# Attention and gated dense block on one core: the exponential table, the last dense bank, two score blocks and the output stores change their places

## The chip, the cores and the metric

The kernel runs on one core of a Trainium2 chip. The metric is the time of one execution in device microseconds, as the median of several runs. The profile comes from one further execution of the same program. The engines are called TensorE (PE; PEld is its weight load), VectorE (DVE), ScalarE (ACT), GpSimd (POOL) and SyncE (SP, which here only issues transfers).

## What is computed

S = 2048 tokens, D = 512 channels, 32 heads of 16 channels, a hidden width F = 1376, all in 32-bit floats:

```python
xn = layernorm(x)
q, k, v = split_heads(xn @ wqkv)             # 32 heads of 16
p = softmax(q @ k.T / 4)                      # 2048 x 2048 a head
s = merge_heads(p @ v) @ wo
g = silu(gelu(xn @ w1 + b1, approximate) @ w2 + b2)
return x + s * g
```

Products with the weights are made from operands split into a high part (rounded to the format of TensorE's fast 32-bit mode) and a low part, in three matmuls each; q and k are stored in both parts too.

## The kernel before

**Units, blocks and steps.** Heads are handled in 8 groups of four (`NG`, `GH`), queries in 4 chunks of 512 (`NCH`); a *unit* `u` is one group with one chunk, 32 in all. The softmax needs each query's maximum before its exponentials. So every unit is passed twice: a max pass, in which TensorE makes 64 *score blocks* of 128 queries x 512 keys (L193) and VectorE reduces each (L199), and an attention pass of 16 *steps*, one for each 128 keys. A step makes four tiles of transposed scores (L714, letters T), turns them into exponentials on ScalarE (one tile each by L717, two together by L719), and adds the value products of the step before (L785, letter V). Of the 2048 score blocks, `SOON` are made in the dense stage and the rest in the attention steps, three in most of them. `due(n)` (L939) says how many are to be done after step `n`; its term `min(FEW, n // 16)` drops one block in the first step of each of the first `FEW` units.

**The dense stage** comes ahead of the attention steps. An order written out by a small planner (`plan`) goes through value tiles (`first`), halves of pairs of units (`half`: two blocks of the first dense layer or of q and k, L583), and parts of the second dense layer (`down`, whose four banks `PA` add up over a chunk of 512 tokens). A half ends with `evac`: ScalarE takes the banks (L368 with the activation function, L370 without, for q and k), rounds them to the high part (L374), and GpSimd subtracts for the low part. The pairs end with a q-k pair, behind which three `down` parts remain. `fill` (L559) puts the score blocks between the matmuls (*rows*): a block may come when `row >= 2 * FILL0 + APART * made`, up to `SOON`.

**The hand-over.** Before the last but one `down` part ScalarE loads the table with the exponential (L731); before the last part TensorE makes the four score tiles of step 0 early (L735). After the last part VectorE adds b2 to the four banks of the last chunk in the order 0, 2, 1, 3 (L643), and GpSimd stores them to `g_d`. Banks 0 and 2 then serve the double tile `two`, bank 1 the value products `pv`, bank 3 the tile `pst` of the later steps. The orders of the first two steps stand in L999; step 1 is `TSTTSVT`.

**The attention steps** take their operation letters from `ORDER`, `FIRST` and `TWO` (S, X and Y are score blocks, H and W parts of the output projection). Work of other engines hangs on step numbers by `at(n, function, ...)`: the key loads by GpSimd (`load_k`, L121), the maxima (L246 to L276), and behind each unit `o_move` (copies the unnormalised output and denominators by SyncE), `o_den` (reciprocal, store of the denominators to `den_d`, and their load back, spread over rows, to `dn`, L813 to L817) and `o_div` (GpSimd multiplies, L823). Each queue goes in program order: an instruction of SyncE or GpSimd that waits holds up all behind it. Key buffers go round three groups (`KB`): group 3 gets the buffer of group 0 and is loaded in halves at steps 56 to 61 and 64 to 69. In group 3's first unit the max pass goes through the keys chunk by chunk.

**The output projection** begins at step `DONE` = 493, beside the last attention steps. Tokens are taken in tiles of 128; tiles 0 to 9 (`NW`; called *tokens* 0 to 9 in the code) go in pairs of two, every four steps: `w_two` splits two channel blocks into `oh` and `ol` (L890 or L892, L893), `w_halves` multiplies with Wo (L912), `load_gx` fetches g and x of a tile (L841, L842), `gate` makes the sigmoid by tanh (L846, L847), `w_gate` and `w_add` (L918, L923) finish, and SyncE stores to `out` (L924). The first ten tiles share four buffers `gx`; a load waits until the tile that had the buffer before is stored. Tiles 10 to 15 have places of their own and come after the last step.

## Time and profile before

| what | us |
|---|---|
| median of 3 runs | 1549.02 (1548.08 to 1549.08) |
| the profiled execution | 1548.39 |
| its span, first to last instruction | 1546.6 |
| VectorE's maxima (L199), 2048 of 687 ns | 1318.0 busy |
| value products (L785), 4096 matmuls | 543.4 busy |
| wide exponentials (L719), 511 of 1018 ns | 520.1 busy |
| first attention steps | from about 469 |
| output projection | from about 1467 |

A row of a timeline has the start, the duration (both us), the engine, the line, the operation, what is written and read, how many instructions are merged in the row, and in brackets the idle time of the engine before it with what ended it. A row of the chain that ended last has start, duration and what the time was spent in. Durations of neighbours overlap, since the engines pipeline; the spacing of starts is what a row costs. A row of a table by stretches has the busy us (and count) of PE, PEld, DVE, ACT and POOL, then the granted TensorE clock as a share of full speed, the DMA share and GB/s.

### The profile page before, as it was taken

How to read it: one execution, taken by the hardware profiler on the slowest of the kernel's cores; microseconds unless marked ns; L12 is line 12 of the kernel's file. 1: busy time of each engine (PE TensorE's matmuls, PEld its weight loads, DVE VectorE, ACT ScalarE, POOL GpSimd, SP SyncE). 2: the span in 40 equal slices, each digit the busy share in tenths (PEclk: the TensorE clock that was granted, in tenths of full speed). 3: DMA queues.
4: the chain of work that ended last, by engine and by line, in shares of the span. 5: the costliest groups of instructions: out<-in, count | busy, mean ns of one | idle time of the engine just before them, and what ended most of it. 6: DMA issues, size and time to landing. Idle time of an engine off the chain costs nothing.

```text
span 1546.6 us, 31293 instructions
## 1 busy us (share of the span) xinstructions
PE 1540.3 (100%) x12232; PEld 923.3 (60%) x12232; DVE 1417.6 (92%) x2295; ACT 1211.8 (78%) x1881; POOL 366.2 (24%) x370
## 2 busy tenths in 40 slices
PE   9999999999999999999999999999999999999999
PEld 8889999999995444444444444444444444444456
DVE  7699999999998999999999999999999999999945
ACT  4333433333329999999999999999999999999984
POOL 4235575756741002001000100100010000000143
PEclk9999999999999999999999999999999999999999
DMA  6525443454432113113311411411041111110153
GB/s 211 154 59 149 124 144 102 128 161 132 137 90 66 41 33 71 33 37 54 67 33 33 71 35 39 63 40 30 22 82 29 33 30 30 43 30 21 48 189 127
DMA packets 78643, 116.83 MB, mean 76 GB/s; under 512 B 28036, under 2 KB 28292, under 8 KB 77320
## 3 DMA queue, kind: packets, MB, share of 16 engines
q1 hardware_dynamic: 74748, 101.89, 23.3%
q0 software_dynamic: 3264, 12.35, 4.7%
q8 instruction: 96, 1.57, 0.4%
q10 hardware_dynamic: 484, 0.60, 0.1%
q14 instruction: 51, 0.42, 0.1%
HBM read 84.35 MB, written 25.97 MB: 71 GB/s over the span
## 4 chain that ended last, share of the span: by engine, by line
PE 97%; DVE 1%; DMA 1%; ACT 0%; SPq 0%; POOL 0%; issue 0%; POOLq 0%; DVEq 0%
PE pv L785 32%; PE ps L193 22%; PE ps L583 13%; PE two L714 8%; PE sp L583 5%; PE pst L714 4%; PE ps L714 4%; PE pst L583 3%; PE pv L583 2%; PE ps L912 1%; PE ps L92 1%; PE ps L455 1%; PE pv L487 1%; PE pst L92 0%; DMA den_d<-dr 0%; PE two L92 0%
## 5 line engine op out<-in xcount | busy, mean ns | idle before, releaser
L199 DVE TENSOR_REDUCE mx<-ps 128x2 f32<-128x512 f32 x2048 | 1318.0, 687 | 69.8 <-PE ps L193 20.5
L785 PE MATMUL pv<-slot,vsb 128*32 128x512 f32 x4096 | 543.4, 604 | 0.0
L719 ACT ACTIVATE slot<-two 128x1024 f32<-128x1024 f32 x511 | 520.1, 1018 | 0.0
L193 PEld LDWEIGHTS ps<-kt,slot 48*128 48x128 f32 x1358 | 212.8, 184 | 291.8 <-DVE mx L199 280.1
L193 PE MATMUL ps<-kt,slot 48*128 48x256 f32 (+1 forms) x1358 | 377.3, 365 | 0.0
L717 ACT ACTIVATE slot<-ps 128x512 f32<-128x512 f32 x515 | 307.6, 598 | 15.7 <-PE ps L714 6.2
L717 ACT ACTIVATE slot<-pst 128x512 f32<-128x512 f32 x511 | 309.0, 605 | 0.6 <-PE ps L714 0.6
L583 PE MATMUL ps<-slot,w1h 64*128 64x512 f32 x1088 | 224.4, 392 | 0.0
L193 PE MATMUL ps<-kt,qz 48*128 48x512 f32 x512 | 202.0, 395 | 0.0
L714 PE MATMUL two<-qt,kt 50*128 50x512 f32 x766 | 197.8, 395 | 0.5 <-DVE gt L643 0.3
L714 PE MATMUL ps<-qt,kt 50*128 50x512 f32 x387 | 189.8, 492 | 0.0
L193 PEld LDWEIGHTS ps<-slot,slot 48*128 48x128 f32 x590 | 92.8, 184 | 123.2 <-DVE mx L199 118.2
L193 PE MATMUL ps<-slot,slot 48*128 48x256 f32 (+1 forms) x590 | 165.4, 366 | 0.0
L785 PEld LDWEIGHTS pv<-slot,vsb 128*32 128x32 f32 x4096 | 81.6, 108 | 132.1 <-issue 124.3
L583 PEld LDWEIGHTS ps<-slot,w1h 64*128 64x128 f32 x1088 | 153.5, 185 | 9.7
L714 PE MATMUL pst<-qt,kt 50*128 50x512 f32 x383 | 156.0, 407 | 0.0
L583 PE MATMUL ps<-slot,w1l 64*128 64x512 f32 x544 | 155.8, 392 | 0.0
L375 POOL TENSOR_TENSOR hl<-hg,hh 128x512 fp32r<-128x512 f32 x76 | 96.7, 1295 | 158.5 <-ACT hh L374 117.1
L368 ACT ACTIVATE hg<-ps,b_sb 128x512 f32<-128x512 f32 x44 | 27.9, 685 | 132.8 <-PE ps L583 121.5
L714 PEld LDWEIGHTS two<-qt,kt 50*128 50x128 f32 x766 | 114.7, 186 | 1.7 <-DVE gt L643 0.7
L193 PEld LDWEIGHTS ps<-kt,qz 48*128 48x128 f32 x512 | 93.7, 183 | 0.9 <-DVE mx L199 0.5
L246 POOL CAST mh<-nt 128x32 fp32r<-128x32 f32 x19 | 4.0, 211 | 361.5 <-DVE nt L244 334.9
(194 smaller groups left out, 1962.5 us busy)
## 6 DMA issues: line engine op xcount, KB each, us to landing
raw<-in_w SPq DMA_DIRECT2D x88, 256.0 KB
qk_h<-hh SPq DMA_DIRECT2D x32, 256.0 KB
qk_l<-hl SPq DMA_DIRECT2D x32, 256.0 KB
qt<-qk_h SPq DMA_DIRECT2D x128, 64.0 KB
slot<-qk_h SPq DMA_DIRECT2D x92, 64.0 KB
g_d<-gt POOLq DMA_DIRECT2D x16, 256.0 KB, 3.3
qt<-qk_l SPq DMA_DIRECT2D x64, 64.0 KB
dn<-den_d SPq DMA_DIRECT2D x32, 128.0 KB
```

The lines of the kernel that those rows point to most:

```text
L92: nc.tensor.matmul(ps, lhs[a], rhs[b], start=first and n == 0, stop=last and n == 2)
L193: return nc.tensor.matmul(ps[:, c0:c0 + w], QS[u][r, p, qi * P:(qi + 1) * P], kts[u // NCH % KB][p][r, k0:k0 + w], start=True, stop=True).ins
L199: nc.vector.tensor_reduce(MX[u][:, 2 * p:2 * p + 2, qi, ki][:, heads, parts], ps.rearrange("p (n c) -> p n c", c=HC), axis=AX.X, op=OP.max)
L368: nc.scalar.activation(raw, ph.pop(u), AF.Gelu_apprx_tanh, bias=b1_sb[:, u[2]:u[2] + 1])
L375: nc.gpsimd.tensor_sub(hl, raw, hh.bitcast(F32))
L455: nc.tensor.matmul(pq["q", g, c], W1[g][i][:, k * P:(k + 1) * P], (xh, xl)[j][c][:, k], start=n == 0 and k == 0, stop=n == 2 and k == KT - 1)
L487: nc.tensor.matmul(pw[:, :P], ident, ident, start=True, stop=True)
L583: i = nc.tensor.matmul(ps, lhs[r], rhs[r], start=first, stop=last).ins
L714: nc.tensor.matmul(ps, kts[g % KB][p][r, k * P:(k + 1) * P], QT[u][r, p, :], start=True, stop=True)
L717: nc.scalar.activation(PT[u, k][:, 2 * p + a, :], ps, AF.Exp, scale=SCALE)
L719: nc.scalar.activation(PT[u, k][:, :2], TP["two"], AF.Exp, scale=SCALE)
L785: nc.tensor.matmul(PV[u][32 * j:32 * j + 32, :], vsb[:, k, h:h + 32], PT[u, k][:, j, :], start=(k == 0), stop=(k == NT - 1))
```

## The change

Six things are moved:

- The load of the exponential's table stands behind the first half of the last q-k pair instead of ahead of the last but one `down` part.
- The last chunk's bank 3 is copied by ScalarE, and GpSimd adds b2 to the copy; VectorE keeps the other three. Step 1 takes the order `TSTTSTV`, with its fourth score tile ahead of the value products.
- `FILL0` goes from 8 to 2, `SOON` from 588 to 590 and `FEW` from 15 to 17.
- The keys of group 3 are loaded in two quarters and a half, from step 52 on.
- The load of the denominators becomes a function of its own, `o_dn`, one or two steps behind `o_den`; the division of the last unit but one comes a step later.
- In the projection, both splits of tiles 0 and 1 are made by GpSimd alone at steps 486 and 488 (before: 491 and 492, with the second copy on ScalarE), tiles 0 to 7 are stored by GpSimd, and tiles 8 and 9 get their rows in the place of a key buffer.

```diff
@@ -34,15 +34,15 @@
 NW = 10
 EARLY = 4
 DONE = 493
-FILL0 = 8
+FILL0 = 2
 APART = 5
 HB = 4
 W2B = 2
 ORDER = {0: "TTTTV", 2: "TSTTSTV", 3: "XTSTTYSTV"}
 FIRST = "STXTTSYTV"
 TWO = ("HTTTTHWV", "TTTTHHV")
-SOON = 588
-FEW = 15
+SOON = 590
+FEW = 17
 SIDES = ((1, 1), (0, 0), (0, 1), (1, 0))
 HC = CH // 2
 PAIRED = 26
@@ -639,7 +639,7 @@
         if f == FT - 1:
             for t in (0, 2, 1, 3):
                 gt = wk.tile([P, D], F32, name="gt", bufs=4)
-                if c == NCH - 1:
+                if c == NCH - 1 and t < 3:
                     nc.vector.tensor_add(gt, PA[c][t], b2_sb)
                 else:
                     nc.scalar.activation(gt, PA[c][t], AF.Copy)
@@ -647,6 +647,8 @@
                 if c < NCH - 1:
                     chores.append((gt, rs))
                 else:
+                    if t == 3:
+                        nc.gpsimd.tensor_add(gt, gt, b2_sb)
                     nc.gpsimd.dma_start(g_d[rs, :], gt)
 
     def chore():
@@ -722,13 +724,13 @@
     for n, e in enumerate(plan):
         if e[0] == "half":
             half(*e[1:])
+            if e[1:] == (len(pairs) - 1, 0):
+                nc.scalar.activation(mhw, b1_sb[:1, :1], AF.Exp)
         elif e[0] == "first":
             quad(*e[1:])
             if e[1:] == (0, 2):
                 ask_qs(1)
         else:
-            if e[1] == parts[-2]:
-                nc.scalar.activation(mhw, b1_sb[:1, :1], AF.Exp)
             if e[1] == parts[-1]:
                 for i in range(EARLY):
                     t_one(0, 0, i)
@@ -812,6 +814,8 @@
         dr = DR.pop(u)
         nc.vector.reciprocal(dr, dr)
         nc.sync.dma_start(den_d[u].rearrange("j (a i) -> (j a) i", i=GH * CH // P), dr)
+
+    def o_dn(u):
         DN[u] = wb.tile([P, CH], F32, name="dn", bufs=1)
         r0 = o_rows(u, 0)[0].start
         nc.sync.dma_start(DN[u][r0:r0 + GH * DH],
@@ -832,7 +836,7 @@
 
     def load_gx(t):
         i = 2 * (t % NCH)
-        if t < NW:
+        if t < NW - 2:
             GX[t] = wb.tile([P, 2, D], F32, name="gx", bufs=4)
         elif t < NT - NCH:
             GX[t] = home(KB)[:, i:i + 2]
@@ -886,7 +890,7 @@
         c, i = divmod(t, NCH)
         src = ot[c][:, k0:k0 + 2, i * P:(i + 2) * P]
         hi, lo = [w.rearrange("p (k t) s -> p k (t s)", t=2) for w in (oh, ol)]
-        if t or k0:
+        if t:
             nc.scalar.activation(hi, src, AF.Copy)
         else:
             nc.gpsimd.tensor_copy(hi, src)
@@ -921,7 +925,7 @@
     def w_add(t, eng, i=0):
         gx, cs = GX[t], cols(t)[i]
         eng.tensor_add(gx[:, 0, cs], gx[:, 0, cs], gx[:, 1, cs])
-        nc.sync.dma_start(out[t * P:(t + 1) * P, cs], gx[:, 0, cs])
+        (nc.gpsimd if t < NW - 2 else nc.sync).dma_start(out[t * P:(t + 1) * P, cs], gx[:, 0, cs])
 
     def w_out(t, eng):
         w_gate(t)
@@ -942,8 +946,9 @@
         g, c = divmod(u, NCH)
         if c == 0 and g == KB:
             for i in range(6):
-                at(56 + i, load_k, g, (i,), nc.gpsimd, 0, S // 2)
-                at(64 + i, load_k, g, (i,), nc.gpsimd, S // 2, S // 2)
+                at(52 + i // 2, load_k, g, (i,), nc.gpsimd, 0, CH)
+                at(56 + i // 2, load_k, g, (i,), nc.gpsimd, CH, CH)
+                at(64 + i // 2, load_k, g, (i,), nc.gpsimd, S // 2, S // 2)
         elif c == 0 and g > KB:
             for i in range(6):
                 at(64 * (g - KB + 1) + 6 + i, load_k, g, (i,), nc.gpsimd)
@@ -956,7 +961,8 @@
         if u < NU - 1:
             at(16 * u + 17, o_move, u, pos=0)
             at(16 * u + (25 if u < NU - 2 else 19), o_den, u, pos=0)
-            at(16 * u + (31 if u < NU - 2 else 22), o_div, u, nc.gpsimd)
+            at(16 * u + (27 if u < NU - 2 else 20), o_dn, u)
+            at(16 * u + (31 if u < NU - 2 else 23), o_div, u, nc.gpsimd)
     T3 = range(NT - NCH, NT)
     late = range(NW, NT)
     for t in range(NW):
@@ -964,7 +970,7 @@
         at(n - 3 + t % 2, load_gx, t)
         if t % 2 == 0:
             for i in range(2):
-                at(n + i - 2, w_two, t, 2 * i)
+                at(n + i - 2 if t else n + 2 * i - 7, w_two, t, 2 * i)
             for i in range(4):
                 for j in range(2):
                     at(n + i, w_halves, t, i % 2 * 2 + j, i // 2, pos="H")
@@ -992,7 +998,7 @@
             for u in list(ended):
                 if u >= PAIRED or ka > 2 and since.setdefault(u, n) < n:
                     s_end0(u)
-        order = TWO[n % 2] if n >= DONE else ORDER[want] if n > 1 else ("TTTTV", "TSTTSVT")[n]
+        order = TWO[n % 2] if n >= DONE else ORDER[want] if n > 1 else ("TTTTV", ORDER[2])[n]
         if want == 3 and ka == 0:
             order = FIRST
         for op in order:
@@ -1021,6 +1027,7 @@
     w_mul(late[0], KS)
     w_chunk(0, nc.gpsimd)
     o_den(NU - 1)
+    o_dn(NU - 1)
     w_out(late[0], nc.vector)
     w_chunk(1, nc.vector)
     w_mul(late[1], KS)
```

## The prediction

> **What bounds the kernel now.** I read the page first (engine totals, the chain that ended last), then busy time by 20 us stretches, then the timelines of single engines where a stretch departs from its neighbours.
>
> ```profile
> PE 1540.3 (100%) x12232; PEld 923.3 (60%) x12232; DVE 1417.6 (92%) x2295; ACT 1211.8 (78%) x1881; POOL 366.2 (24%) x370
> PE 97%; DVE 1%; DMA 1%; ACT 0%; SPq 0%; POOL 0%; issue 0%; POOLq 0%; DVEq 0%
> 100.00:120.00 20.00, 20.00 (x174) 17.89 (x172) 19.64 (x30) 5.72 (x11) 11.38 (x9) 1.00 0.36 112
> ```
>
> TensorE holds 97% of the chain, at a granted clock of 1.00 (the column after POOL). In the dense stage it passes 174 matmuls in 20 us, 0.115 us each. So its work costs what it costs wherever it stands, and this change hardly alters that work. What can be won or lost are TensorE's waits, and I looked for them at the four places that the diff touches: the hand-over from the dense stage to attention, the two score blocks that change stage, the keys of group 3, and the output projection beside the last attention steps.
>
> **The hand-over.** ScalarE, then TensorE, then VectorE, in order of time:
>
> ```profile
> 463.80 1.09 ACT L370 ACTIVATE hg<-ps 128x512 f32<-128x512 f32 x2 [7.16 <-PE ps L583]
> 465.94 1.28 ACT L731 ACT_TABLE_LOAD   x1
> 467.35 2.48 ACT L717 ACTIVATE slot<-ps 128x512 f32<-128x512 f32 x5
> 469.86 1.02 ACT L719 ACTIVATE slot<-two 128x1024 f32<-128x1024 f32 x1
> 471.51 0.60 ACT L717 ACTIVATE slot<-pst 128x512 f32<-128x512 f32 x1 [0.63 <-PE ps L714]
> ```
>
> ```profile
> 466.48 0.39 PE L714 MATMUL ps<-qt,kt 50*128 50x512 f32 x1
> 469.31 0.50 PE L714 MATMUL two<-qt,kt 50*128 50x512 f32 x2 [0.28 <-DVE gt L643]
> 469.98 1.07 PE L785 MATMUL pv<-slot,vsb 128*32 128x512 f32 x8
> 470.98 0.50 PE L714 MATMUL pst<-qt,kt 50*128 50x512 f32 x1
> 472.59 1.06 PE L785 MATMUL pv<-slot,vsb 128*32 128x512 f32 x8
> 474.60 1.06 PE L785 MATMUL pv<-slot,vsb 128*32 128x512 f32 x8
> ```
>
> ```profile
> 467.97 1.29 DVE L643 TENSOR_TENSOR gt<-sp,b_sb 128x512 f32<-128x512 f32 x2 [1.92 <-PE sp L583]
> 469.17 0.68 DVE L643 TENSOR_TENSOR gt<-pv,b_sb 128x512 f32<-128x512 f32 x1
> 469.77 0.68 DVE L643 TENSOR_TENSOR gt<-pst,b_sb 128x512 f32<-128x512 f32 x1
> ```
>
> Now the table load runs after the last roundings, from 465.94, and the first exponential starts at 467.35 although its scores (TensorE, 466.48 + 0.39) were there at 466.87. In the changed order the load stands behind the first half of the last q-k pair. ScalarE idled 7.16 us ahead of 463.80, so 1.28 us there are covered; without that cover the load would push the roundings and cost what it costs today. The exponentials can then start at 466.87, 0.48 us earlier. That time is spent again: the fourth dense bank's copy is new on ScalarE, ahead of step 1's exponentials. From 467.35 to 469.86 five exponentials passed, 0.50 each; now four, the copy and one more make six from 466.87, and the wide exponential starts at 466.87 + 6 x 0.50 = 469.87, as today. VectorE loses the add at 469.77, which nobody else needs early; the add of b2 on GpSimd and its store have no reader for a millisecond.
>
> The gain comes behind that. Today step 1 issues its fourth score tile (pst, 470.98) behind the value products (469.98); ScalarE idles 0.63 us for it, its exponential starts at 471.51, and the next value products at 472.59, 2.61 us after the first; the pair after that is 2.01 apart (474.60), which is a step's normal length. In the changed order this tile comes before the value products. Its bank is free when the copy ends, at 466.87 + 5 x 0.50 = 469.37 and some tenths; the value products wait for the bank that VectorE empties until 469.85 in any case. So they start at 469.98, or up to 0.2 later if the tile isn't hidden, and the next ones 2.01 later: 472.0 to 472.2 instead of 472.59. **I take -0.5** (bounds -0.6 and, if the copy is the last to come, 0).
>
> **Two score blocks go from the attention steps to the dense stage.**
>
> ```profile
> 53.56 0.39 PE L193 MATMUL ps<-kt,qz 48*128 48x512 f32 x1
> 48.70 0.42 SPq L121 DMA_DIRECT2D kt<-qk_l  x1
> kt<-qk_h POOLq DMA_DIRECT2D x8, 128.0 KB, 4.3
> 664.60 1.02 ACT L719 ACTIVATE slot<-two 128x1024 f32<-128x1024 f32 x1
> 890.83 1.02 ACT L719 ACTIVATE slot<-two 128x1024 f32<-128x1024 f32 x1
> 1053.06 1.02 ACT L719 ACTIVATE slot<-two 128x1024 f32<-128x1024 f32 x1
> 1280.44 1.02 ACT L719 ACTIVATE slot<-two 128x1024 f32<-128x1024 f32 x1
> ```
>
> SOON 590 puts two more blocks into the dense stage: 2 x 0.115 = **+0.23**. FILL0 2 lets the first come at row 4 instead of row 16, so the last ends at row 4 + 5 x 589 = 2949 against 16 + 5 x 587 = 2951, and no block moves into the hand-over. Twelve rows are 1.4 us: the first block comes at about 52.2 instead of 53.56. Its last key load was issued at 48.70; no row times its landing, the nearest is 4.3 us for twice the bytes (128 KB), so it can be there between 51 and 53, and a stall of 0 to 0.8 us is possible. I take 0, since the block that reads the last three loads comes five rows later.
>
> FEW 17 gives two more units of 16 steps 47 score blocks instead of 48 (units 16 and 17). Its price is read from the starts of the wide exponential, one a step: steps 97 to 209 are seven units with 47 blocks and take 890.83 - 664.60 = 226.23, 32.32 a unit; steps 289 to 401, with 48, take 227.38, 32.48. So 2 x 0.164 = **-0.33** (bounds 0 and -0.4).
>
> **Keys of group 3 in quarters.**
>
> ```profile
> 582.50 0.51 POOL L121 DMA_DIRECT2D kt<-qk_l  x1
> 593.69 1.02 ACT L719 ACTIVATE slot<-two 128x1024 f32<-128x1024 f32 x1
> 595.87 1.02 ACT L719 ACTIVATE slot<-two 128x1024 f32<-128x1024 f32 x1
> ```
>
> The step from 593.69 to 595.87 takes 2.18 instead of 2.01: it is where score blocks first read group 3. The last load of that half was issued at 582.50 and with 4.3 us to landing was there by 587.3, six us before. So it isn't late data, and loading a quarter earlier can't mend it; I read the 0.17 as what a step pays for taking over freshly loaded keys. Three portions instead of two mean one more such step: **+0.1** (bounds -0.17 if it was late data after all, and +0.17). GpSimd issues 18 loads instead of 12, at half a microsecond each, with 24% of its time used; the first now waits for step 51's products, and what queues behind it on GpSimd is due at step 63.
>
> **The output projection.** First its start:
>
> ```profile
> 1469.66 0.19 PEld L912 LDWEIGHTS ps<-wo_h,ol 64*128 64x128 f32 x2 [0.57 <-POOL ol L893]
> 1467.82 0.21 POOL L246 CAST mh<-nt 128x32 fp32r<-128x32 f32 x1 [32.36 <-DVE nt L244]
> 1468.32 1.29 POOL L893 TENSOR_TENSOR ol<-slot,oh 128x512 fp32r<-128x512 f32 x1
> ```
>
> TensorE waits 0.57 us for the low parts of tokens 0-1, channels 256-511 (1468.32 + 1.29 = 1469.61). GpSimd could not make them sooner: ahead in its queue stood the last unit's maxima, for which it idled 32.36 us. Placed at step 488, with its copy on GpSimd too, this work falls into those 32 us. **-0.55** (bounds -0.6 and 0).
>
> Then its third pair of tokens:
>
> ```profile
> 1488.31 4.42 DMA den_d<-dr
> 1493.38 4.06 DMA gx<-g_d
> 1497.47 0.63 ACT L846 ACTIVATE slot<-gx 128x512 f32<-128x512 f32 x1 [1.53 <-DMA gx<-g_d]
> 1494.41 1.04 ACT L719 ACTIVATE slot<-two 128x1024 f32<-128x1024 f32 x1
> 1504.05 1.02 ACT L719 ACTIVATE slot<-two 128x1024 f32<-128x1024 f32 x1
> 1515.64 1.02 ACT L719 ACTIVATE slot<-two 128x1024 f32<-128x1024 f32 x1
> ```
>
> SyncE's queue stands for 4.42 us because the load of the denominators waits for their own store; the gate rows of token 5 are issued behind it, at 1493.38, need 4.06 us, and ScalarE idles 1.53 us for them, then TensorE for ScalarE. The steps show the price: 1494.41 to 1504.05 are three steps in 9.64, while the four to 1515.64 take 2.90 each; 9.64 - 3 x 2.90 = 0.94. The change takes the denominators' load one step later, behind these rows, and takes the output stores of tokens 0-7 out of this queue. **-0.95** (bounds -0.95 and 0, below). In the earlier units the same split frees SyncE, but no row of TensorE or ScalarE waits for it there: 0.
>
> What GpSimd pays:
>
> ```profile
> 1480.04 2.55 POOL L923 TENSOR_TENSOR gx<-gx 128x512 f32<-128x512 f32 x2
> 1487.82 1.29 POOL L893 TENSOR_TENSOR ol<-slot,oh 128x512 fp32r<-128x512 f32 x1 [5.22 <-PE ps L714]
> 1521.18 1.34 POOL L858 TENSOR_TENSOR ol<-ot,oh 128x512 fp32r<-128x512 f32 x1 [2.52 <-ACT oh L857]
> 468.96 2.33 POOL L650 DMA_DIRECT2D g_d<-gt  x4 [0.87 <-DVE gt L643]
> ```
>
> Its two adds of a pair end at 1482.59 and its next work starts 5.2 us later; before the last pair that gap is 2.52. Four stores of the same size took 2.33 at 468.96, 0.58 each, so two add 1.2 and fit. Tokens 8 and 9 take their rows from another buffer, so their loads no longer wait for the stores of 4 and 5.
>
> **The sum.** -0.5 + 0.23 - 0.33 + 0.1 - 0.55 - 0.95 = -2.0 us. The profiled execution took 1548.39 (span 1546.6 and 1.8 around it), so its like would take 1546.4. The median of the runs shown, 1549.02, lies 0.63 above that execution; I predict medians: **1547.0**.
>
> **The rivals.** *A new wait for token 5's rows.* Their buffer is free once token 1's store has landed; that store now leaves from GpSimd, at about 1482.6 - 0.55 + 1.2 = 1483.2. With 4.3 to land and 4.06 for the load the rows are there at 1491.6; ScalarE wants them at 1497.47 - 1.53 = 1495.9, or 1495.4 after the gain before. It takes 3.8 us more, under the traffic of that stretch, to lose the 0.95: 1547.9. Chance 0.12.
>
> *The hand-over gains nothing*, since copy and exponentials fill ScalarE: 1547.5. Speaks for it that my two starts of the wide exponential agree within 0.01, with no slack left. 0.06.
>
> *GpSimd is held by its stores: slower.* If a store kept GpSimd until it has landed, 4.06 us as the loads need there, two would take 8.1 against gaps of 5.2 (three pairs) and 2.52 (one): 3 x 2.9 + 5.6 = 14.3 us late for the low parts, all of it on TensorE if it has no lead: 1561.3. It decides from 2.6 us a store on (1.26 before the last pair). Against it stand the four stores in 2.33 us, beside three VectorE instructions of the rows above. 0.08. The Trainium skill (SBUF — State Buffer, section "A bandwidth-pool intuition that's wrong (but worth ruling out)") speaks for it: GpSimd writes the descriptors of its own transfers and can't while VectorE holds their common port; it tells of a transfer of 620 ns that became 3100 beside a copy. By that figure the loss would be 3 x 1.0 + 3.7 = 6.7 and the time an estimated 1553.7. The trace does not agree for the additions that VectorE ran beside the stores at 468.96, 0.58 each; no row here shows a store beside VectorE's work of the projection.
>
> *Everything falls on the good side*: the two blocks free in the dense stage, the keys' 0.17 gone, -0.6 and -0.6 where I took less: -0.6 - 0.33 - 0.17 - 0.6 - 0.95 = -2.65, and the spread of the runs (1548.08 to 1549.08) adds half a microsecond: 1545.9 or below. 0.15.
>
> **How the numbers follow.** My forecast, 1546.0 to 1547.8, has 0.59. Two parts in a thousand are 3.1 us, about what a measurement of this kernel tells from no change, so faster means below 1545.9 and slower above 1552.1. Faster 0.15 (the last rival), slower 0.08 (GpSimd held), the rest, 0.77, in between. The range leaves out the slower rival and most of the fastest case, and takes in the two that lose one gain and a late first block: 1545.4 to 1549.0.
>
> **What would show it.** Right: the table load near 456 to 458 with no later idle on ScalarE because of it; step 1 to step 2 near 2.0 instead of 2.62 by the wide exponential's starts; units 16 and 17 at 32.3; two to three steps of about 2.1 to 2.2 around steps 61 to 75; no wait of TensorE at the first projection tiles; steps 502 to 504 at 2.9 each. Wrong: a gap ahead of the first score block near 52; GpSimd's stores longer than 1 us; ScalarE waiting for gate rows of another token, which would mean that the wait has only moved.

## The result, and the profile after

The changed kernel takes **1546.69 us** (median of 20 runs, 1546.34 to 1547.21); the kernel before took 1548.72 beside it (20 runs, 1547.91 to 1549.55). The ratio is 0.9987, with a 95% interval of 0.9981 to 0.9993: faster by 2.03 us, where -2.0 was forecast. The span of the profiled execution went from 1546.6 to 1544.6.

The page of the changed kernel, engine totals and chain, and its table by stretches:

```profile
PE 1538.4 (100%) x12230; PEld 922.5 (60%) x12230; DVE 1419.2 (92%) x2294; ACT 1212.4 (78%) x1881; POOL 375.8 (24%) x386
PE 99%; DVE 1%; DMA 0%; issue 0%; ACT 0%; DVEq 0%
100.00:120.00 20.00, 20.00 (x176) 18.20 (x173) 19.61 (x29) 6.01 (x11) 11.38 (x9) 1.00 0.35 110
```

TensorE's share of the chain went from 97% to 99%, and DMA's from 1% to 0%: waits went, and work stayed. The dense stretch shows 176 matmuls where 174 stood; score blocks are 29 of them in both kernels.

**Where the 2 us are.** I cut the span by the starts of the wide exponential, one a step, as the prediction did, and the dense stage by its first and last matmul. Us before and after:

| stretch | before | after | difference |
|---|---|---|---|
| up to the first dense matmul | 51.61 | 51.49 | -0.12 |
| dense stage, to its last matmul | 416.79 | 417.18 | +0.39 |
| from there to step 3's wide exponential | 6.22 | 5.88 | -0.34 |
| steps 3 to 81 | 157.60 | 157.61 | +0.01 |
| steps 81 to 241 | 323.45 | 323.28 | -0.17 |
| steps 241 to 273 (with the first steps of units 16 and 17) | 64.85 | 64.52 | -0.33 |
| steps 273 to 492 | 445.08 | 444.94 | -0.14 |
| steps 492 to 495 | 8.53 | 8.12 | -0.41 |
| steps 495 to 502 | 20.28 | 20.27 | -0.01 |
| steps 502 to 505 | 9.64 | 8.69 | -0.95 |
| steps 505 to 511 | 17.39 | 17.38 | -0.01 |

The differences add up to -2.08; the span differs by 2.0. The rest is rounding and what lies behind step 511 (25.2 us in both).

The first row is noise: it lies ahead of everything that was changed, and in the profiles below it goes from 51.49 to 52.30. So kernels are compared by stretches here, more closely than whole times allow. Each kernel has one profile, and the spread of a stretch is read from the kernels that leave it alone. It is 0.02 for steps 492 to 495 and 0.01 for steps 502 to 505, but 0.18 for steps 81 to 241 and 0.26 for steps 273 to 492. So the -0.14 of steps 273 to 492 is no more than noise.

**The hand-over.** ScalarE of the changed kernel, in order of time:

```profile
456.38 1.28 ACT L728 ACT_TABLE_LOAD   x1
457.67 0.20 ACT L728 ACTIVATE mhw<-b_sb 1x1 f32<-1x1 f32 x1
464.29 1.08 ACT L370 ACTIVATE hg<-ps 128x512 f32<-128x512 f32 x2 [5.89 <-PE ps L583]
467.49 2.06 ACT L719 ACTIVATE slot<-ps 128x512 f32<-128x512 f32 x4 [1.08 <-PE ps L716]
469.41 0.63 ACT L645 ACTIVATE gt<-pst 128x512 f32<-128x512 f32 x1
470.36 1.09 ACT L721 ACTIVATE slot<-two 128x1024 f32<-128x1024 f32 x1
472.54 1.02 ACT L721 ACTIVATE slot<-two 128x1024 f32<-128x1024 f32 x1
```

The table load is at 456.38, and 5.89 us of idle time still stand behind it: it is covered. The first exponential starts at 467.49, later than the 467.35 of before, but the whole dense stage ends 0.27 later here: counted from the last dense matmul it is 0.13 earlier. L645 is the new copy of bank 3. Steps 1 and 2, by the wide exponentials, now start 2.18 apart (470.36 to 472.54) instead of 2.62. TensorE over the same time:

```profile
466.78 0.39 PE L716 MATMUL ps<-qt,kt 50*128 50x512 f32 x1
468.67 0.39 PE L583 MATMUL pst<-w2h,hl 64*128 64x512 f32 x1
469.60 0.50 PE L716 MATMUL two<-qt,kt 50*128 50x512 f32 x2 [0.31 <-DVE gt L643]
470.10 0.49 PE L716 MATMUL pst<-qt,kt 50*128 50x512 f32 x1
470.52 1.06 PE L787 MATMUL pv<-slot,vsb 128*32 128x512 f32 x8
472.52 1.06 PE L787 MATMUL pv<-slot,vsb 128*32 128x512 f32 x8
```

468.67 is the last dense matmul (468.40 before). The tile `pst` (470.10) comes ahead of the value products now. These start at 470.52, 1.85 us behind the last dense matmul (1.58 before), and again 2.00 later (2.61 before). Together 3.85 instead of 4.19.

**The projection.** PEld at the first low parts, VectorE's gate product, and GpSimd's stores:

```profile
1466.91 0.31 PEld L916 LDWEIGHTS ps<-wo_h,ol 64*128 64x128 f32 x2
1480.87 2.13 DVE L851 SCALAR_TENSOR_TENSOR gx<-slot,gx 128x512 f32<-128x512 f32 x1 [2.26 <-ACT slot L850]
1480.53 0.62 POOL L928 DMA_DIRECT2D out<-gx  x1 [0.30 <-POOL gx L927]
1481.16 1.28 POOL L927 TENSOR_TENSOR gx<-gx 128x512 f32<-128x512 f32 x1
1482.74 0.57 POOL L928 DMA_DIRECT2D out<-gx  x1 [0.30 <-POOL gx L927]
```

TensorE loads `ol` at 1466.91 without a wait. Each output store takes GpSimd about 0.6 us. SyncE's queue and the gate of token 5:

```profile
1486.54 0.32 SPq L845 DMA_DIRECT2D gx<-g_d  x1
1489.74 0.59 SPq L821 DMA_DIRECT2D dn<-den_d  x1
1494.67 0.67 ACT L850 ACTIVATE slot<-gx 128x512 f32<-128x512 f32 x1
```

The gate rows of token 5 are issued at 1486.54 (1493.38 before), ahead of the denominators' load at 1489.74, and ScalarE's gate at 1494.67 waits for nothing.

### The profile page after: what moved, and what is told of

It reads as the page before. It is cut to its first block, busy times and chain, and to the rows that moved or that the text cites. A ratio compares the mean times of both kernels' runs of the same rounds, so it can differ in the third digit from the quotient of the medians.

```text
span 1544.6 us, 31302 instructions
## 1 busy us (share of the span) xinstructions
PE 1538.4 (100%) x12230; PEld 922.5 (60%) x12230; DVE 1419.2 (92%) x2294; ACT 1212.4 (78%) x1881; POOL 375.8 (24%) x386
## 4 chain that ended last, share of the span: by engine, by line
PE 99%; DVE 1%; DMA 0%; issue 0%; ACT 0%; DVEq 0%
PE pv L787 33%; PE ps L193 22%; PE ps L583 13%; PE two L716 8%; PE sp L583 5%; PE ps L716 4%; PE pst L716 4%; PE pst L583 3%; PE pv L583 2%; PE ps L916 2%; PE ps L92 1%; PE ps L455 1%; PE pst L92 0%; DVE st L414 0%; PE two L92 0%; DMA xt<-in_x 0%
```

## The experiments

All twelve kernels are the changed kernel with one part of it undone or one thing added. Lines of a diff with "-" are the changed kernel, those with "+" the experiment. Each was timed against the kernel before on the same chip; the ratios below are to that kernel. Whole times can't tell ten of the twelve from the changed kernel (ratios 0.9985 to 0.9993, each with an interval of about 0.0009 to either side, and 0.9987 for the changed kernel). So the prices are lengths of stretches. The steps' lengths are taken from the starts of the wide exponential, as in the table.

### The third pair of tokens: which of two parts frees SyncE?

My theory was one queue: SyncE issues in order, and token 5's rows stood behind the load of the denominators and the stores. Either part alone might do. In `no_split` that load goes back behind its store; in `sync_stores` SyncE keeps all stores; `neither` undoes both.

```diff
no_split:
-            at(16 * u + (27 if u < NU - 2 else 20), o_dn, u)
+            at(16 * u + (25 if u < NU - 2 else 19), o_dn, u, pos=0)
sync_stores:
-        (nc.gpsimd if t < NW - 2 else nc.sync).dma_start(out[t * P:(t + 1) * P, cs], gx[:, 0, cs])
+        nc.sync.dma_start(out[t * P:(t + 1) * P, cs], gx[:, 0, cs])
neither: both
```

> The changed kernel, but the load of the denominators is back in one go with their store (steps 25 and 19 of a unit as before). Theory 'one queue': the wait at the third pair of tokens came from two things that stood in SyncE's queue ahead of token 5's gate rows, the output stores of tokens 0 and 1 (they held the copies of the unnormalised output back until 1483.05) and the denominators' load; either removal alone is enough. It expects no return of the wait: steps 502 to 504 take 8.7 us together, time as the changed kernel within 0.3 us (1546.7). Rival 'the split alone': the denominators' load is what held the rows; steps 502 to 504 take 9.6 and the time rises by 0.95.

> The changed kernel, but tokens 0 to 7 are stored by SyncE as before; the split of the denominators' store and load stays. Theory 'one queue' expects steps 502 to 504 at 8.7 us, since token 5's rows now stand ahead of the denominators' load, and the time as the changed kernel within 0.3. Rival 'the stores alone': the rows come too late as long as SyncE waits for GpSimd's adds; 9.6 and 0.95 slower.

> The changed kernel with both undone: the denominators' load in one go with their store, and all stores by SyncE. Tokens 8 and 9 keep their new place. Theory 'one queue': the wait is back, steps 502 to 504 at 9.6 us, time 0.95 above the changed kernel (1547.6). Rival 'another place': the new place of the rows of tokens 8 and 9, or the earlier splits of tokens 0 and 1, removed the wait; then 8.7 and no change.

Measured: `no_split` 1547.13, ratio 0.9987 (0.9978 to 0.9995), steps 502 to 505 in 8.68 us; `sync_stores` 1547.05, 0.9985 (0.9976 to 0.9994), 8.69; `neither` 1548.26, 0.9993 (0.9984 to 1.0001), 9.90. SyncE's queue in the three, in this order; `gx<-g_d` are token 5's rows:

```profile
1489.23 0.59 SPq L821 DMA_DIRECT2D dn<-den_d  x1
1489.92 0.39 SPq L845 DMA_DIRECT2D gx<-g_d  x1
```

```profile
1480.96 1.59 SPq L928 DMA_DIRECT2D out<-gx  x2
1488.33 0.43 SPq L845 DMA_DIRECT2D gx<-g_d  x1
1492.72 0.59 SPq L821 DMA_DIRECT2D dn<-den_d  x1
```

```profile
1481.27 1.59 SPq L928 DMA_DIRECT2D out<-gx  x2
1492.93 0.59 SPq L821 DMA_DIRECT2D dn<-den_d  x1
1493.57 0.45 SPq L845 DMA_DIRECT2D gx<-g_d  x1
1497.65 0.63 ACT L850 ACTIVATE slot<-gx 128x512 f32<-128x512 f32 x1 [1.78 <-DMA gx<-g_d]
```

In `no_split` the rows still stand behind the denominators' load, but without the two stores (they leave at 1481.27 in `neither`, behind GpSimd's additions, and take 1.59 us) the rows go out 3.65 us earlier than in `neither`, and 1489.92 is early enough. In `sync_stores` the stores are back, but the rows pass the load, which stands until 1492.72. Only with both undone do the rows leave at 1493.57, and ScalarE idles 1.78 us for them. Either part takes the wait away, and the second then brings nothing measurable. The theory holds; its price is 9.90 - 8.69 = 1.2 us. The steps take 0.26 more than in the kernel before (9.64), and what adds that is open.

### The projection's start

`two_late` puts both splits of tokens 0-1 back to steps 491 and 492, with the second copy on ScalarE; `two_scalar` keeps the early place and gives only that copy back to ScalarE.

```diff
two_late, both lines; two_scalar, the first:
-        if t:
+        if t or k0:
-                at(n + i - 2 if t else n + 2 * i - 7, w_two, t, 2 * i)
+                at(n + i - 2, w_two, t, 2 * i)
```

> The changed kernel, but tokens 0 and 1 are split as before: steps 491 and 492, the second copy on ScalarE. Theory 'queue behind the maxima': GpSimd reaches the second low part only after the last unit's maxima, TensorE waits again; from the start of the wide exponential of step 492 to that of step 495 it takes 8.5 us instead of 8.1, time 0.43 up. Rival 'ScalarE': it is the copy on ScalarE that pushed the exponentials of step 493, and the low part's wait is the smaller share; then ScalarE idles no less ahead of the first exponential of step 494 and the time rises by under 0.2.

> The changed kernel with the splits of tokens 0 and 1 at the early steps 486 and 488, but the second copy on ScalarE as before. Theory 'the place': what the projection's start gained came from standing ahead of the last unit's maxima in GpSimd's queue; from step 492 to 495 it stays at 8.1 us. ScalarE is busy 19.8 of 20 us in these steps, so its 0.5 us of copy show in steps 488 to 491: 0.3 to 0.5 more there. Rival 'slack': the attention steps are TensorE's, and the copy is absorbed; no change anywhere.

Measured: `two_late` 1547.42, ratio 0.9989 (0.9979 to 0.9998); steps 492 to 495 take 8.55, and 8.12 in the changed kernel: +0.43. ScalarE of `two_late`, and TensorE's load of the low parts:

```profile
1465.33 1.02 ACT L721 ACTIVATE slot<-two 128x1024 f32<-128x1024 f32 x1
1466.71 0.64 ACT L894 ACTIVATE oh<-slot 128x512 fp32r<-128x512 f32 x1
1467.71 1.05 ACT L721 ACTIVATE slot<-two 128x1024 f32<-128x1024 f32 x1
1469.39 0.19 PEld L916 LDWEIGHTS ps<-wo_h,ol 64*128 64x128 f32 x2 [0.58 <-POOL ol L897]
```

`two_scalar` 1547.49, 0.9990 (0.9981 to 0.9998); steps 492 to 495 take 8.13, so nothing is lost there, but steps 481 to 492 take 22.67 instead of 22.31. Timeline of ScalarE in `two_scalar`:

```profile
1457.37 1.02 ACT L721 ACTIVATE slot<-two 128x1024 f32<-128x1024 f32 x1
1458.75 0.64 ACT L894 ACTIVATE oh<-slot 128x512 fp32r<-128x512 f32 x1
1459.75 1.05 ACT L721 ACTIVATE slot<-two 128x1024 f32<-128x1024 f32 x1
```

The copy (L894) pushes the next exponentials: the step from 1457.37 to 1459.75 takes 2.38 instead of 2.01. In `two_late` the same happens in step 492, as in the kernel before: with the copy (1466.71) it takes 2.38 (1465.33 to 1467.71) instead of 2.01, ahead of TensorE's wait for the low parts (0.58, at 1469.39). Steps 493 and 494, in which that wait lies, take 6.17 together, against 6.11. So by these lengths the copy on ScalarE makes 0.37 of the 0.43 and the wait 0.06: the rival 'ScalarE' has the larger part, though it put the total too low. The early place with the copy left on ScalarE gains only 0.43 - 0.36 = 0.07. No run has the late place with the copy on GpSimd, so what the place is worth there stays open. ScalarE has no room for 0.5 us in a step; GpSimd idled for 30.

### The hand-over: which edit carries the gain?

Three kernels undo one part each. `table_late` loads the table ahead of the last but one `down` part again, `old_order` gives step 1 the order `TSTTSVT` again, `vector_bank` lets VectorE add b2 to all four banks again.

```diff
table_late:
-            if e[1:] == (len(pairs) - 1, 0):
-                nc.scalar.activation(mhw, b1_sb[:1, :1], AF.Exp)
...
+            if e[1] == parts[-2]:
+                nc.scalar.activation(mhw, b1_sb[:1, :1], AF.Exp)
old_order:
-        order = ... else ("TTTTV", ORDER[2])[n]
+        order = ... else ("TTTTV", "TSTTSVT")[n]
vector_bank:
-                if c == NCH - 1 and t < 3:
+                if c == NCH - 1:
...
-                    if t == 3:
-                        nc.gpsimd.tensor_add(gt, gt, b2_sb)
```

> The changed kernel, but the exponential's table is loaded at its old place, ahead of the last but one part of the second layer. Measured from the start of the last dense matmul (pst, w2h with hl) to the start of step 3's wide exponential: 6.22 us before, 5.88 in the changed kernel. Theory 'ScalarE's chain': the fourth tile of step 1 and with it the first value products wait for the copy of bank 3, which stands behind the four early exponentials; with the load of 1.28 and 0.2 behind the last roundings these start 0.4 later, so 6.3 and the time 0.4 up. Rival 'VectorE's banks': the value products wait for the bank that VectorE empties anyway; then at most 0.1 is lost.

> The changed kernel, but step 1 has its old order, the fourth score tile behind the value products. From the last dense matmul to step 3's wide exponential: 5.88 in the changed kernel. Theory 'ScalarE's chain': the value products start earlier (by 0.3, when VectorE's bank is free), but the fourth tile comes 1.0 later and ScalarE waits for it; 6.2, time 0.3 up. Rival 'table load alone': the gain of the hand-over comes from the table load and the order is worth nothing; 5.9.

> The changed kernel, but VectorE adds b2 to all four banks as before, so ScalarE has no copy; the new order of step 1 and the early table load stay. From the last dense matmul to step 3's wide exponential: 5.88 in the changed kernel. Theory 'ScalarE's chain': the fourth tile now waits for VectorE's fourth add, which ends 0.6 behind the third, 0.65 later than the copy; 6.5, time 0.6 up: the new order needs the copy. Rival: ScalarE, 0.5 shorter, starts the wide exponential earlier and makes up for it; 5.9.

Measured, with the time from the last dense matmul to the second value products (before 4.19, changed 3.85):

| kernel | us, ratio | last dense matmul | second value products | between |
|---|---|---|---|---|
| table_late | 1547.37, 0.9988 (0.9979 to 0.9997) | 469.09 | 473.28 | 4.19 |
| old_order | 1547.53, 0.9987 (0.9978 to 0.9996) | 469.48 | 473.67 | 4.19 |
| vector_bank | 1547.67, 0.9988 (0.9979 to 0.9997) | 468.81 | 473.36 | 4.55 |

Up to step 3's wide exponential it is 6.22, 6.21 and 6.57 (changed 5.88): the same losses, 0.3 and 0.7. Each edit is needed, and the gain of 0.34 is that of all three. With `old_order` the early table gives nothing, since ScalarE waits for the late tile again. With `table_late` the whole gain is spent on the later exponentials:

```profile
466.91 1.28 ACT L733 ACT_TABLE_LOAD   x1
468.31 2.00 ACT L719 ACTIVATE slot<-ps 128x512 f32<-128x512 f32 x4
```

And in `vector_bank` the new order and the early table without the copy are worse than before by 0.36. TensorE waits for VectorE's fourth add ahead of the tile that now stands ahead of the value products:

```profile
470.92 0.50 PE L714 MATMUL pst<-qt,kt 50*128 50x512 f32 x1 [0.46 <-DVE gt L643]
```

### The hand-over: earlier tiles

The first exponential of the changed kernel waits for its scores (467.49, 1.08 us idle). `early_tiles` makes tiles 0 and 1 of step 0 ahead of the last but one `down` part.

```diff
-            if e[1] == parts[-1]:
-                for i in range(EARLY):
+            if e[1] in parts[-2:]:
+                for i in ((0, 1), (2, 3))[parts.index(e[1]) - len(parts) + 2]:
```

> A further step beyond the changed kernel: tiles 0 and 1 of step 0 are made ahead of the last but one part of the second layer, tiles 2 and 3 ahead of the last as now. Theory 'ScalarE's chain': the first two exponentials run from 466.4, right behind the last roundings, so the copy of bank 3 starts when its bank is complete (469.1) instead of 469.41 and the fourth tile 0.3 earlier; from the last dense matmul to step 3's wide exponential 5.6 instead of 5.88, time 0.3 down. Rival 'VectorE's banks': the value products wait for VectorE in any case; 5.85 and no change.

Measured: 1547.12, ratio 0.9986 (0.9977 to 0.9994); from the last dense matmul of bank `pst` (469.19; one of another bank follows at 469.25) to the second value products (473.06) 3.87. No gain, as the rival has it. The exponentials do start earlier, and the time is then lost twice:

```profile
466.83 1.08 ACT L719 ACTIVATE slot<-ps 128x512 f32<-128x512 f32 x2
469.71 0.60 ACT L645 ACTIVATE gt<-pst 128x512 f32<-128x512 f32 x1 [0.39 <-PE pv L583]
```

```profile
470.40 0.50 PE L716 MATMUL two<-qt,kt 50*128 50x512 f32 x2 [0.53 <-DVE gt L643]
```

ScalarE's copy waits for the last dense matmuls (0.39), and the double tile waits 0.53 for VectorE's adds. So behind ScalarE stand the dense matmuls and VectorE's banks, and an earlier start alone can't be cashed in.

### GpSimd held by its stores

The slower rival had a deciding point: 2.6 us a store. `hold_3us` puts two subtractions of 1.29 us, whose result nobody reads, behind each of the eight stores on GpSimd.

```diff
+        if not JUNK:
+            JUNK.append(wb.tile([P, D], F32, name="junk", bufs=1))
         (nc.gpsimd if t < NW - 2 else nc.sync).dma_start(out[t * P:(t + 1) * P, cs], gx[:, 0, cs])
+        if t < NW - 2:
+            for _ in range(2):
+                nc.gpsimd.tensor_sub(JUNK[0], wo_h[:, 0].bitcast(F32), wo_l[:, 0].bitcast(F32))
```

> The changed kernel, but behind each of the eight stores GpSimd makes two subtractions that nobody reads (1.29 us each), so that a store holds GpSimd for 0.58 + 2.58 = 3.16 us: the slower rival of the prediction, made by hand. In the changed kernel GpSimd idles 3.40, 1.79, 3.10 and 0.78 us between a pair's work and the next low part; 5.16 us more a pair overrun these gaps by 1.8, 3.4, 2.1 and 4.4. Theory 'lead': TensorE uses a low part some 2 us after it is made, so only about 3 us of this 11.6 reach it, and the time rises by 2 to 4. Rival 'no lead': all of it, 11.6. Rival 'hidden': the second low part of a pair has 1.6 us of waiting ahead of it that takes up the rest; under 0.5.

Measured: 1557.72, ratio 1.0060 (1.0047 to 1.0072); span 1555.1, which is 10.5 more than the changed kernel's. "No lead" (11.6) is nearer than "lead" (2 to 4). GpSimd's timeline, and from the table of waits between 1474 and 1540 TensorE's own for it (us in total, times, longest):

```profile
1480.98 0.62 POOL L932 DMA_DIRECT2D out<-gx  x1 [0.30 <-POOL gx L931]
1481.62 2.99 POOL L935 TENSOR_TENSOR junk<-wo_h,wo_l 128x512 f32<-128x512 f32 x2
```

```profile
PE ps L916 <- POOL ol L897: 4.2, 3, 2.5
PE pst L92 <- POOL ol L862: 2.0, 1, 2.0
```

A store with its hold takes about 0.58 + 2.99 = 3.6 us. The rival's own sum, 3 x (7.2 - 5.2) + (7.2 - 2.5) = 10.7, is close to the 10.5, but in part by chance. TensorE pays late: steps 492 to 505 lose 0.7 and steps 505 to 511 4.8 (22.17 for 17.38), when GpSimd's queue has fallen behind far enough; 4.6 come behind step 511. And of these 4.6 some are no waiting: from 1532.25 to 1535.66, where the wait of 2.0 ends, the granted clock was 0.50, and TensorE's 3.35 busy us there cost about 1.7 us more than at full clock (an estimate: half of them). So the rival's mechanism exists, and its premise fails: the real store takes 0.6 and not 4.

### The two score blocks and the keys

`fill_old` gives the fill its old constants, `keys_halves` loads group 3's keys in two halves again.

```diff
fill_old:
-FILL0 = 2
+FILL0 = 8
-SOON = 590
-FEW = 17
+SOON = 588
+FEW = 15
keys_halves:
-                at(52 + i // 2, load_k, g, (i,), nc.gpsimd, 0, CH)
-                at(56 + i // 2, load_k, g, (i,), nc.gpsimd, CH, CH)
-                at(64 + i // 2, load_k, g, (i,), nc.gpsimd, S // 2, S // 2)
+                at(56 + i, load_k, g, (i,), nc.gpsimd, 0, S // 2)
+                at(64 + i, load_k, g, (i,), nc.gpsimd, S // 2, S // 2)
```

> The changed kernel with FILL0 8, SOON 588 and FEW 15 as before. From the prediction: the dense stage (first to last matmul of it) 0.2 to 0.4 us shorter, units 16 and 17 (steps 257 to 272, and 241 to 256 and 273 to 288 beside them) 0.33 longer together, no net change over 0.2. Rival 'fresh keys': the two blocks also shifted the steps at which groups 4 and 5 are first read, where the changed kernel lost 0.15 (step 149) and 0.1 (step 237) less; then these come back too and the time rises by 0.2 to 0.3.

> The changed kernel with the keys of group 3 in halves, as before, at steps 56 to 61 and 64 to 69. Theory 'fresh keys': a step that takes over newly loaded keys pays for it, late or not; step 61 stays at 2.18, the step of the second quarter (67, 2.08) goes back to 2.02, time down by 0.06, too little to be seen in the runs. Rival 'late data': with two blocks more made ahead the halves come too late; step 61 or 72 takes over 2.3 and the time rises by 0.2 or more.

`fill_old`: 1547.34, ratio 0.9988 (0.9979 to 0.9997). Its dense stage takes 416.67 (51.84 to 468.51); the changed kernel and the ten experiments that keep its fill and its early tiles take 416.94 to 417.34, 417.11 in the mean. So the two blocks and the earlier start cost **0.4** there. Steps 241 to 273 take 64.82 again instead of 64.52; steps 81 to 241 323.39 (323.28, and 323.20 to 323.38 in all kernels with the new fill). Steps 273 to 492 take 445.13, within the 444.93 to 445.19 of the kernels with the new fill. What the fill takes in one stage it gives back in the other: +0.4 there, -0.3 and some -0.1 here. In whole times (1.8 us under the kernel before, 2.0 for the changed kernel) the two can't be told apart.

`keys_halves` was the surprise: **1550.39, ratio 1.0006 (0.9997 to 1.0015)**, span 1548.3, 3.7 more than the changed kernel. Steps 49 to 81 take 68.11 instead of 64.81: the 3.3 us lie in step 62 (4.42 instead of 1.99) and step 63 (2.98 instead of 2.02). GpSimd, TensorE, and TensorE's busy time with the granted clock (the number behind the count) there:

```profile
580.07 1.05 POOL L121 DMA_DIRECT2D kt<-qk_h  x2 [21.83 <-PE pst L716]
592.25 0.50 POOL L121 DMA_DIRECT2D kt<-qk_l  x1 [9.65 <-PE pst L716]
```

```profile
591.49 0.46 PE L193 MATMUL ps<-kt,slot 48*128 48x512 f32 x1
595.35 0.47 PE L193 MATMUL ps<-kt,slot 48*128 48x512 f32 x1 [1.58 <-DMA kt<-qk_l]
```

```profile
593.20:596.61 3.41, 1.83 (x16) 1.00 0.14 38
596.61:600.02 3.41, 3.41 (x20) 0.50 0.00 0
```

The sixth load of the half waits 9.65 us for TensorE and leaves at 592.25; the score block at 595.35 waits 1.58 for it. That is half of the loss. From 1.3 us behind the wait's end the granted clock was 0.50 for 3.41 us, all of them busy: work that takes half of that at full clock, so about 1.7 us more (an estimate). The runs fit this: eight of the eleven have a mean clock of 0.999 and took 1550.05 or more, three have 1.000 and took 1548.85 to 1549.16; the profile is of one of the eight. The cause of the wait is the order in the program. Blocks are made in pairs, and the steps here have three: half a pair (X with Y) and a whole one (both S). `due(60)` is 590 + 179 - 3 = 766 with the new fill, 383 pairs. So step 61 takes pair 383, the last of group 2, for X and Y, and pair 384, the first of group 3 (12 units of 32), for its two S. The row at 591.49 is the second S: it reads `kt`, as no block of the kernel before does before step 62, where the old fill (`due(60)` = 764, 382 pairs) puts pair 384. But the sixth load hangs on step 61 too, behind the fourth tile. Now it comes after a block that reads its place, must wait until that block is done (the profile names the tile `pst` of the same moment, which in step 61 reads keys of the other half, so this step is argued from the program), and the next block must wait for the load. (That one block takes its maxima with the low part of the older keys in this kernel.) In the changed kernel the first quarter's loads hang on steps 52 to 54. In GpSimd's timeline they start at once when the place is free, and no load of the second quarter waits for a score block either:

```profile
571.84 1.06 POOL L121 DMA_DIRECT2D kt<-qk_h  x2 [14.03 <-PE pst L716]
```

"Late data" had the sign, and neither theory the cause or the size. The quarters don't shorten any step by themselves; they are what lets `SOON` be 590. Halves with the old fill are the kernel before, 64.82 in these steps, and quarters with the old fill are `fill_old`, 64.82 too.

## Why the prediction was right, point by point

- **The hand-over** (-0.5 taken, bounds -0.6 and 0; measured 4.19 to 3.85 = -0.34). The mechanism was right, and the size was off in one step: "The exponentials can then start at 466.87, 0.48 us earlier." Their scores ended at 466.78 + 0.39 = 467.17, and the first exponential began 0.32 behind that, at 467.49; before it began 0.48 behind. So only 0.16 were gained there, and the copy, the tile and the value products came later by the rest. The sentence "So they start at 469.98, or up to 0.2 later" named the place: it is 1.85 - 1.58 = 0.27 later. Why a first exponential starts 0.3 behind the modelled end of its scores no run tells.
- **Bank 3's copy** ("as today" for the wide exponential) is fair: six instructions from 467.49 to 470.36, 0.48 each. The rival "hand-over gains nothing" is wrong, but close: `table_late` and `old_order` show it as soon as one edit is missing.
- **Two blocks more in the dense stage** (+0.23; measured +0.4). Right in sign; the fill costs about 0.2 a block there, not 0.115 (no run has the two blocks without the earlier start). The first block came at 52.07 without a gap, so the feared stall of 0 to 0.8 didn't come.
- **FEW 17** (-0.33; measured -0.33), by `fill_old` too (-0.30).
- **The keys** (+0.1; measured 0.0 over steps 49 to 81). The step in which group 3 is first read still takes 2.18, one step earlier (step 61), so "it isn't late data, and loading a quarter earlier can't mend it" is right. But the part was judged against the old fill only. With the new one the quarters are worth 3.3 us in the profiles, about half of it the wait and half the clock behind it, a dependence between two parts of the change that I hadn't worked out, though `due` and the steps of the loads give it by counting.
- **The projection's start** (-0.55; measured -0.41, by `two_late` 0.43). The size is near, and the mechanism was mostly another. The step that failed is "TensorE waits 0.57 us for the low parts", taken whole as the price. The wait is there and goes, but by the lengths of steps it cost about 0.06. The other 0.37 were the copy on ScalarE, which the prediction moved ("with its copy on GpSimd too") without a term for it. That the two sums are near each other is luck.
- **The third pair** (-0.95; measured -0.95). Right, to the hundredth; the runs add that either of the two parts is enough.
- **GpSimd pays nothing** (0; measured 0 over steps 495 to 502 and 505 to 511): stores of 0.56 to 0.62 against 0.58 predicted. The rival "GpSimd is held" falls with that. The figure of the Trainium skill (SBUF — State Buffer, section "A bandwidth-pool intuition that's wrong (but worth ruling out)"), which it gives for a VectorE copy, does not carry over to this case: a store that starts just before a VectorE product, at 1480.53, takes 0.62. `hold_3us` shows that such a hold would have cost about what the rival's sum gives, part of it by the clock.
- **The wait for token 5's rows in a new place** didn't come: issued at 1486.54, wanted at 1494.67.
- **Unpredicted**: -0.17 in steps 81 to 241. The steps in which groups 4 and 5 are first read became shorter (steps 149 and 237, from 2.17 and 2.10 to 2.02 and 2.01); with `fill_old` step 149 takes 2.18 again. So it comes with the fill; what shortens them is open.

That the sum came out to the tenth is partly luck. Two terms were taken 0.15 too large as gains (hand-over, projection's start) and one 0.15 too small as a cost. Against them stand 0.1 for the keys that wasn't paid, 0.17 in the steps of the fill that I hadn't seen, and 0.26 of noise (the first row and steps 273 to 492). The third pair, half of the gain, was right in mechanism and size.

## What to carry to other kernels

A transfer behind a waiting one in an in-order queue may be freed by any one of several edits ahead of it, as here by either of two. So price such edits together, and expect that the second may bring nothing. An experiment that undoes two things prices both, and the lengths of single steps tell which one paid. When work is moved a step earlier, count which loads it now passes in the program: a load that comes after the reader of its place waits for that reader, and everything behind it waits too. A wait of TensorE can cost twice here, since the clock may be lower behind it (0.50 in `keys_halves`). Moving blocks from one stage of a full engine to another is a swap; the gains are in the waits.

## What the runs showed of the hardware

TensorE's granted clock fell to 0.50 behind two waits, for 3.41 us each time. In `keys_halves` TensorE was busy for 1.83 us of the 3.41 ahead (593.20 to 596.61, with the wait of 1.58), and the clock was 0.50 from 596.61 to 600.02. In `hold_3us` it was busy for 1.49 us of the 3.41 ahead (1528.84 to 1532.25, with a wait of 2.0), and the clock was 0.50 from 1532.25 to 1535.66. The other kernels show no such stretch beside the first 8 us and the last 2 of their spans. A longer wait in `hold_3us`, 2.5 us up to 1506.14, left it at 1.00; what decides it, these cases don't show.

VectorE's gate product (L851, two inputs from the on-chip memory SBUF) takes 0.69 us alone, as at 1483.42 in the changed kernel. When a GpSimd addition or multiplication had begun before it and ran on for 0.3 us or more, it ended 0.54 to 0.56 us behind that one's end. `sync_stores`, whose two additions run without stores between them, VectorE first and then GpSimd:

```profile
1481.59 1.15 DVE L851 SCALAR_TENSOR_TENSOR gx<-slot,gx 128x512 f32<-128x512 f32 x1 [2.25 <-ACT slot L850]
1479.63 2.55 POOL L927 TENSOR_TENSOR gx<-gx 128x512 f32<-128x512 f32 x2
```

The product ends at 1482.74 and the addition at 1482.18, and the product takes 1.15. When the product began first, it was GpSimd that took longer: in `fill_old` the product starts at 1495.87 and takes 0.69, and the multiplication at 1495.88 takes 1.85 instead of 1.29. The rule of the Trainium skill that fits (SBUF — State Buffer, section "SBUF: two separate sides") is that the port which the two engines share is held by one instruction as a whole, the one that starts first.

One pair is different, in every kernel that stores from GpSimd. In the changed kernel's rows above the product starts at 1480.87, ahead of the addition at 1481.16, and still ends 0.56 behind it: 1480.87 + 2.13 = 1483.00, and 1481.16 + 1.28 = 1482.44. A GpSimd store (1480.53, 0.62) was running when the product started; whether that store held the port, no run tells. It makes the product 1 us longer than in `sync_stores`, off the path in this kernel.

The load of the exponential's table took 1.28 us, and the next activation began 0.01 us behind it: 456.38 + 1.28 = 457.66 against 457.67, the small exponential of L728 that asks for the table, in the rows of ScalarE above.
